# A second two-layer token group goes to seven products for eight, in halves of 256 tokens

## Chip, cores and metric

The kernel runs on one core of one Trainium2 chip. The metric is device time in microseconds of one execution. Three timed executions of the kernel before gave 1100.1, 1101.35 and 1101.55 us; their median is 1101.35 us. One more execution was profiled, and every row below is from that one.

## What is computed

Attention over 4 batches, 8 heads, 576 tokens and 64 columns per head, with scores under (row maximum − tau) left out, and then two dense layers over 2304 tokens of width 512, each with 2048 hidden columns:

```python
def reference(**kwargs):
    attn_out = _attn_ref(**attn_kwargs)
    x = attn_out.transpose(0, 2, 1, 3).reshape(B * S, H * D)
    h = x @ w_in                                      # layer 1
    g = np.where(h >= 1, h, np.where(h <= -1, 0.0, (h + 1) ** 2 / 4))
    x = g @ w_out
    h = x @ w_in2                                     # layer 2
    g = h * np.clip(h + 3.0, 0.0, 6.0) / 6.0
    return g @ w_out2
```

## The kernel before

Everything is held as pairs: an fp32 value is split into a high part (fp32r) and the rest, "low" (`wih`/`wil`, `xh`/`xl`, `gh`/`gl`), and each product of two values is three matmuls (high·high, high·low, low·high). The tokens lie in five groups: four of 512 (one per batch, 0 to 3) and one of 256 (group 4, the last 64 tokens of each batch). The attention and most of layer 1 run first; the change lies in layer 2, from about 716 us on.

Layer 2 before has these stages, in order:

1. Plain groups: `dense(1, 3, ...)` over groups 3, 4 and 0 (`order3`), 16 blocks f of 128 hidden columns each. A step is an input product of 12 matmuls (`em_h`, L725), the gate on ScalarE and VectorE, the split of the gate's result into `gh` (ScalarE) and `gl` (GpSimd), and, two steps later, the output product, 24 matmuls for 512 tokens and 6 for group 4 (`em_out`, L767). `ahead3` puts the layer's weight loads and weight sums beside the steps.
2. The pair: `unit()`. Groups 1 and 2 are the two column halves of one matrix product; two blocks f make its row halves and 256 of the 512 input columns its inner halves. So 2x2 blocks are multiplied with seven products for eight (`PRODUCTS`, L1362: 7 products of 6 matmuls of 512 columns for each of 8 pairs p of blocks). Their left sides are the weights' blocks and sums of them, which `combine` makes in stage 1 and stores to DRAM (`sd`); `fetch` brings them back through a ring of 12 tiles. Their right sides (`combos`, `xw`) are made by `prepare` and lie where the layer's input weights lay. ScalarE copies partial results out of the PSUM banks (`p1`, `U2`, `U3`), VectorE adds the rest (`C11`, `C21`, `C22`, `C12`), and the gate follows. Group 1's gate results go on to its output product (`outs_of`, L1165, one pair of blocks behind); group 2's are stored to DRAM (`rd2`). Beside that, `weight_sums` makes sums of the output weights and stores them (`td`).
3. The last group's output: group 2's output product is done with seven products for eight too (`out_product`, L1300, 336 matmuls of 256 columns). Its left sides come from `rd2` (`load_pair`, `sum_pair`, `high_pair`, `low_pair`), its right sides from `td` (`fetch_sum`, 32 loads).

A scheduler orders the instructions of each engine from the order of the code and a cost model of its own; `after` adds an order (`pins`). Each engine then works through its instructions in that order. Nearly all transfers are issued by SyncE, in its own order.

## Time and profile before

| what | value |
|---|---|
| median of three timed executions | 1101.35 us (1100.1 to 1101.55) |
| the profiled execution: its time | 1102.58 us |
| its span, first to last instruction | 1100.8 us |
| granted TensorE clock, mean | 0.992 of full speed |
| TensorE matmul busy | 1067.0 us (97%) |
| VectorE, ScalarE, GpSimd busy | 740.7, 656.6, 454.0 us |
| moved by DMA | 140.97 MB |

Busy times are shares of the span; a matmul's end is modelled, so matmuls overlap in the rows: what a stream of them costs is read from the chain's rows, where a piece "2.72 us, x12" is twelve starts in a row.

### The profile page before, as it was taken

The page shows a single profiled execution, that of the slowest core. Times are in us where ns is not written, and L with a number is a line of the kernel's source. Part 1 is how long each engine was busy: PE and PEld are TensorE (multiplying, and loading weights), DVE is VectorE, ACT ScalarE, POOL GpSimd, SP SyncE. Part 2 cuts the span into 40 slices and gives each one's busy share as a digit, 9 for nine tenths or more (in the row PEclk, how much of TensorE's full clock was granted, in tenths as well). Part 3 has the DMA queues.
Part 4 walks back from the last instruction along what each step waited for, and adds up shares of the span by engine and source line. Part 5 has one row for each costly group of instructions (what it writes and reads, how often), then busy time and mean ns, then how long its engine had stood idle before and what let it go on. Part 6 is the DMA issues. An engine that isn't in the chain of part 4 may idle for free.

```text
span 1100.8 us, 18826 instructions
## 1 busy us (share of the span) xinstructions
PE 1067.0 (97%) x6658; PEld 882.2 (80%) x6658; DVE 740.7 (67%) x1432; ACT 656.6 (60%) x1304; POOL 454.0 (41%) x390
## 2 busy tenths in 40 slices
PE   7988889999999999999999999999999999999998
PEld 5555567777888888888889888888898888888888
DVE  5899887976676757256536755458565655778766
ACT  5777887776766767465556666645544333544542
POOL 0233667742222322146636665567723222211242
PEclk9999889999999999999999999999999999999999
DMA  6454446233222221015323555655244412877891
GB/s 170 117 98 101 117 118 149 64 75 88 70 66 66 45 61 44 30 50 172 94 73 125 164 178 164 212 169 154 77 154 151 136 58 67 269 259 250 279 348 39
DMA packets 178190, 140.97 MB, mean 128 GB/s; under 512 B 103088, under 2 KB 144304, under 8 KB 178096
## 3 DMA queue, kind: packets, MB, share of 16 engines
q1 hardware_dynamic: 176176, 138.95, 43.3%
q8 instruction: 52, 0.85, 0.3%
q10 hardware_dynamic: 1920, 0.82, 0.3%
q14 instruction: 42, 0.34, 0.1%
HBM read 93.00 MB, written 46.73 MB: 127 GB/s over the span
## 4 chain that ended last, share of the span: by engine, by line
PE 83%; DVE 8%; DMA 3%; ACT 2%; issue 1%; POOL 1%; SPq 1%; DVEq 0%; ACTq 0%; POOLq 0%
PE Q L725 27%; PE P L767 20%; PE Q L787 7%; PE Q L1362 6%; PE Q L482 6%; PE P L381 5%; PE Q L295 4%; PE P L1165 3%; DVE p L396 3%; DVE p L418 2%; PE P L1300 2%; PE Q L1300 1%; DMA tw<-td 1%; DVE xl L706 1%; SPq L234 1%
## 5 line engine op out<-in xcount | busy, mean ns | idle before, releaser
L743 POOL TENSOR_TENSOR gl<-r,gh 128x256 fp32r<-128x256 f32 (+1 forms) x158 | 167.1, 1058 | 324.6 <-ACT gh L742 312.2
L725 PE MATMUL Q<-xh,wih 128*128 128x256 f32 (+1 forms) x632 | 211.8, 335 | 2.6 <-DVE r L736 2.3
L725 PE MATMUL Q<-xl,wih 128*128 128x256 f32 (+1 forms) x632 | 207.3, 328 | 0.0
L725 PE MATMUL Q<-xh,wil 128*128 128x256 f32 (+1 forms) x632 | 207.2, 328 | 0.0
L736 DVE SCALAR_TENSOR_TENSOR r<-r,Q 128x256 f32<-128x256 f32 (+1 forms) x110 | 54.8, 498 | 124.6 <-ACT r L735 120.8
L418 DVE SCALAR_TENSOR_TENSOR p<-p,th,e 128x576 f32<-128x576 f32 x144 | 127.7, 909 | 15.8 <-ACT e L409 10.0
L725 PEld LDWEIGHTS Q<-xh,wih 128*128 128x128 f32 x632 | 120.1, 190 | 21.0 <-DVE r L736 4.1
L742 ACT ACTIVATE gh<-r 128x256 fp32r<-128x256 f32 (+1 forms) x158 | 79.6, 504 | 86.6 <-DVE r L736 31.1
L409 ACT ACTIVATE e<-p,nm 128x576 f32<-128x576 f32 x144 | 109.4, 775 | 36.2 <-DVE p L396 35.3
L725 PEld LDWEIGHTS Q<-xl,wih 128*128 128x128 f32 x632 | 120.2, 190 | 10.9
L725 PEld LDWEIGHTS Q<-xh,wil 128*128 128x128 f32 x632 | 120.1, 190 | 10.3
L295 PE MATMUL Q<-ident,p 128*128 128x128 f32 x656 | 107.3, 281 | 12.8 <-ACT Gf L446 9.7
L295 PEld LDWEIGHTS Q<-ident,p 128*128 128x128 f32 x656 | 74.0, 141 | 42.4 <-ACT Gf L446 16.1
L144 POOL TENSOR_TENSOR w_c<-w_c,w_raw 128x512 int32<-128x512 int32 x64 | 89.5, 1399 | 39.9 <-DVE w_c L142 20.6
L381 PE MATMUL P<-kt,qt 64*128 64x288 f32 (+2 forms) x508 | 82.8, 412 | 10.1 <-DVE p L396 8.1
L446 ACT ACTIVATE Gf<-Q 128x512 f32<-128x512 f32 x128 | 74.2, 595 | 15.8 <-PE Q L295 15.1
L1362 PE MATMUL Q<-xw,sw 128*128 128x512 f32 x336 | 81.0, 390 | 0.0
L396 DVE TENSOR_SCALAR_CACHE_REDUCE p<-P 128x576 f32<-128x576 f32 x90 | 65.2, 751 | 18.9 <-PE Q L295 11.9
L734 ACT ACTIVATE r<-Q,half 128x256 f32<-128x256 f32 (+1 forms) x110 | 58.5, 534 | 32.2 <-PE Q L725 25.3
L787 PE MATMUL Q<-gh,woh 128*128 128x256 f32 x240 | 75.3, 314 | 1.4 <-DVE ob L800 1.4
L1362 PEld LDWEIGHTS Q<-xw,sw 128*128 128x128 f32 x336 | 62.9, 188 | 13.6 <-DVE C L1388 0.7
L482 PE MATMUL Q<-Gf,vn 128*64 128x320 f32 (+1 forms) x512 | 72.8, 423 | 0.1
(199 smaller groups left out, 2454.5 us busy)
## 6 DMA issues: line engine op xcount, KB each, us to landing
w_raw<-in_moe_w_in_dram SPq DMA_DIRECT2D x32, 512.0 KB
w_raw<-in_moe_w_out_dram SPq DMA_DIRECT2D x32, 512.0 KB
sw<-sd SPq DMA_DIRECT2D x56, 256.0 KB
sd<-wz SPq DMA_DIRECT2D x32, 256.0 KB
td<-tz SPq DMA_DIRECT2D x16, 512.0 KB
tw<-td SPq DMA_DIRECT2D x32, 256.0 KB
vn<-in_v_dram SPq DMA_DIRECT2D x32, 128.0 KB
x2p<-ob SPq DMA_DIRECT2D x16, 256.0 KB
```

Of the source, the lines that this page charges most:

```text
L144: x = G.tensor_tensor(out=c.bitcast(I32), in0=c.bitcast(I32), in1=r, op=ALU.add)
L295: x = T.transpose(out, in_, ident)
L381: mm = T.matmul(o, a[j][r, cs], w[j][r, k0:k0 + HS], start=(n == 0), stop=(n == len(terms) - 1), skip_group_check=True)
L396: reads(V.tensor_scalar(out=p[:, x], in0=s[:, :, 0:HS], scalar1=taus[:, 3:4] if j >= JR else -1.0, scalar2=3e38, op0=ALU.mult, op1=ALU.min ...
L409: pins["S"] = S.activation(out=e, in_=p[:, x], func=ACTF.Exp, bias=nm[:, x:x + 1], scale=-1.0)
L418: pins["M"] = V.scalar_tensor_tensor(out=p[:, x], in0=p[:, x], scalar=th[:, x:x + 1], in1=e, op0=ALU.is_le, op1=ALU.mult, accum_out=zt[j][ ...
L482: mm = T.matmul(o[h * D:(h + 1) * D], vn[j % 2][:, c, h, :], f[:, h, c] if c < 4 else t, start=(c == 0), stop=(c == 4), skip_group_check=True)
L725: mm = T.matmul(h, l[:, kk * 128:(kk + 1) * 128], r, start=(x == 0), stop=(x == 3 * KD - 1))
L743: y = G.tensor_tensor(out=gl, in0=r, in1=f32(gh), op=ALU.subtract)
L767: T.matmul(a, l, r, start=(first and x == 0), stop=(last and x == 2))
L787: mm = T.matmul(o, l, r, start=(f == fs[0] and x == 0 and i == 0), stop=(f == fs[-1] and x == 2 and i == 1), skip_group_check=True)
L1362: mm = T.matmul(banks[role], t[:, l, c, :], r, start=(first and y == 0), stop=(y == 5), skip_group_check=True)
```

## The change

Group 0 leaves the plain groups and becomes a second run of the unit, `unit(True)`, behind the pair: its two halves of 256 tokens are the two column halves. Its products have 256 columns (`combos2`, `xz`, made by `small_load` and `small_step` beside the pair's last blocks). The three groups change roles at the output: groups 1 and 2 are now multiplied plainly (group 2's gate results are read back from `rd2` by `again`, split, and multiplied beside group 0's products), and group 0's gate results, stored as `rd3`, take the seven output products at the end. The weight sums of the first two pairs of blocks are made in front, beside group 3 (`EARLY`), those of the other six beside the pair, with their low parts on GpSimd; the sums' source is a copy in DRAM (`ed`) that ScalarE's queue stores when the weights are split. The output weights' sums are made beside the second unit, low parts on GpSimd; those of pairs 0 to 5 stay on the chip (`home`), and only pairs 6 and 7 go through `td`. `fin_out` lets ScalarE evict the even blocks.

```diff
+    ed = [dram.tile([128, 512], F32, name=f"ed{f}") for f in range(KF)]
+    rd3 = [dram.tile([128, MAIN], F32, name=f"rs{f}") for f in range(KF)]
...
         x = S.activation(out=hi, in_=f32(c), func=ACTF.Copy)
         after(x, pins["S"])
+        if (kind, m) == ("i", 1):
+            nc.scalar.dma_start(out=ed[f], in_=f32(c))
...
     def fin_out(g, a, i):
-        if i % 2:
+        if i % 2 == 0:
             S.activation(out=ob, in_=a, func=ACTF.Copy, scale=1.0 / 6.0)
...
-    order3 = [NB - 1, NB, 0]
+    order3 = [NB - 1, NB]
+    G0 = 0
...
+    def small_part(k, c, t):
+        hi, lo = combos2[c, XN[k]] = small_tile(k, c)
+        paced(S.activation(out=hi, in_=t, func=ACTF.Copy), "S")
+        minus(lo, t, f32(hi))
+    def small_load(c):
+        raw2[c] = [wide["p"].tile([128, MAIN], F32, tag="xst", name="ty", bufs=3) for _ in range(3)]
+        for t, kk in zip(raw2[c], (c, 2 + c)):
+            nc.sync.dma_start(out=t, in_=x2d[G0][:, kk, :])
...
-    def weight_sums():
+    def weight_sums(ps):
+        def home(p):
+            n = 2 + 2 * p if p < 6 else 2 * p - 10
+            return [[place_of(n + x, hl, F32R, "tw") for hl in "hl"] for x in range(2)]
...
-                minus(z[:, 1, :], t, f32(z[:, 0, :]))
-                nc.sync.dma_start(out=f32(td[p])[:, n], in_=f32(z))
+                rounded_off(lo, t, hi, False)
+                for x, t in enumerate((hi, lo)):
+                    if p < 6:
+                        tw[p, 2 * n + x] = t
+                    else:
+                        nc.sync.dma_start(out=f32(td[p])[:, n, x], in_=f32(t))
...
-    def unit():
+    def unit(second, between):
+        n = 256 if second else MAIN
+        xs_of = combos2 if second else combos
...
+            def sink(t, row, col):
+                if second:
+                    r = t[:, 256:512]
+                    S.activation(out=r, in_=t[:, 0:256], func=ACTF.Relu, bias=three)
+                    pins["V"] = V.scalar_tensor_tensor(out=r, in0=r, scalar=6.0, in1=t[:, 0:256],
+                                                       op0=ALU.min, op1=ALU.mult)
+                    nc.sync.dma_start(out=rd3[(f0, f1)[row]][:, 256 * col:256 * col + 256], in_=r)
+                elif col:
+                    nc.sync.dma_start(out=rd2[(f0, f1)[row]], in_=gate(t))
+                else:
+                    gg[(f0, f1)[row]] = parts(gate(t))
+            p1 = copy("p1", product(0, 0), n)
+            sink(add("C11", product(1, 1), p1, n), 0, 0)
+            outs(0)
+            u2 = copy("U2", product(2, 0, False), n)
+            c21 = product(4, 2)
+            outs(1)
+            u3 = copy("U3", product(3, 0, False), n)
+            sink(add("C21", u3, c21, n, ALU.subtract), 1, 0)
+            sink(add("C22", product(5, 3), u3, n), 1, 1)
+            outs(2)
+            outs(3)
+            sink(add("C12", product(6, 3, False), u2, n), 0, 1)
+            between(p, 7)
...
+    def again(f):
+        r = ringed("r", F32)
+        nc.sync.dma_start(out=r, in_=rd2[f])
+        hh[f] = parts(r)
+    def beside_first(p, k):
+        if k < 7:
+            next(late, 0)
+        if p == last_p - 2 and k == 7:
+            small_load(0)
+        elif p == last_p - 1 and k < 6:
+            small_step(k + 1, 0)
...
+    def beside_second(p, k):
+        if k in (2, 4):
+            again(2 * p + (k == 4))
+        if p < last_p:
+            next(sums_of, 0)
+            if k == 7 and p == last_p - 1:
+                load_pair(0)
+                load_pair(1)
+                for n in range(5):
+                    fetch_sum(n)
+            return
...
+    first_sums = in_turn(range(EARLY), True)
+    late = in_turn(range(EARLY, KF // 2), False)
+    sums_of = weight_sums((6, 7, 0, 1, 2, 3, 4, 5))
...
-    unit()
+    unit(False, beside_first)
+    unit(True, beside_second)
+    last_group()
```

What stands in each engine's row of work shows it at three places. `Q` and `P` are PSUM banks, `sw` the fetched weight blocks.

TensorE, in layer 2: before, one step of group 0, an input product and the output products two steps behind.

```order
L725 MATMUL Q_10521<-xl,wih_8940 128x512
L725 MATMUL Q_10521<-xh,wil_8941 128x512
L767 MATMUL P_10151<-woh_8815,gh 128x512
L767 MATMUL P_10151<-wol_8816,gh 128x512
L767 MATMUL P_10151<-woh_8815,gl 128x512
```

And now, in the second unit, the start of one pair of blocks: two products of 256 columns, a part of group 2's output, and two more products, the first into the bank that the first product left.

```order
L1443 MATMUL Q_11852<-xz,sw 128x256 x6
L1443 MATMUL Q_11869<-xz,sw 128x256 x6
L1227 MATMUL P_11455<-woh_8404,gh 128x512
L1227 MATMUL P_11455<-wol_8405,gh 128x512
L1227 MATMUL P_11455<-woh_8404,gl 128x512
L1227 MATMUL P_11455<-woh_8536,gh 128x512
L1227 MATMUL P_11455<-wol_8537,gh 128x512
L1227 MATMUL P_11455<-woh_8536,gl 128x512
L1443 MATMUL Q_11852<-xz,sw 128x256 x6
L1443 MATMUL Q_11907<-xz,sw 128x256 x6
```

Group 0's 192 input matmuls of 512 columns became 336 of 256; all other counts in layer 2 stay (384 of 512 columns at L1165 and L767 for the outputs of two groups are now at L1227).

GpSimd, in the pair before (all of it rests of gate results):

```order
L1154 TENSOR_TENSOR gl_11413<-r_11409,gh_11412 128x512
L1154 TENSOR_TENSOR gl_11499<-r_11495,gh_11498 128x512
L1154 TENSOR_TENSOR gl_11555<-r_11551,gh_11554 128x512
L1154 TENSOR_TENSOR gl_11641<-r_11637,gh_11640 128x512
L1154 TENSOR_TENSOR gl_11691<-r_11687,gh_11690 128x512
```

And at the start of the second unit, where `gl_11319`, `11357`, `11473`, `11512` are the rests of group 2's blocks f = 0 to 3 and `gl_11618` that of f = 4:

```order
L1216 TENSOR_TENSOR gl_11319<-r_11316,gh_11318 128x512
L1216 TENSOR_TENSOR gl_11357<-r_11354,gh_11356 128x512
L1095 TENSOR_TENSOR tw_11361<-te_11279,tw_11360 128x512
L1095 TENSOR_TENSOR tw_11363<-te_11292,tw_11362 128x512
L1216 TENSOR_TENSOR gl_11473<-r_11470,gh_11472 128x512
L1216 TENSOR_TENSOR gl_11618<-r_11615,gh_11617 128x512
L1216 TENSOR_TENSOR gl_11512<-r_11509,gh_11511 128x512
L1095 TENSOR_TENSOR tw_11490<-te_11424,tw_11489 128x512
```

The low parts of the weight sums (`tw`) stand between the rests, and block 3's rest stands behind block 4's.

ScalarE, where the last pair of blocks begins: before, the last group's first split (`gt`) stood behind the copies `p1` and `U2` of that pair.

```order
L1147 ACTIVATE r_11725<-C12_11723,three_75 128x512
L1383 ACTIVATE p1_11760<-Q3_11753 128x512
L1147 ACTIVATE r_11778<-C11_11776,three_75 128x512
L1383 ACTIVATE U2_11809<-Q3_11753 128x512
L1153 ACTIVATE gh_11781<-r_11778 128x512
L1259 ACTIVATE gt_11799<-r2_11735 128x256
```

Now it stands ahead of both, and of the gate of `C12` of the pair of blocks before.

```order
L1215 ACTIVATE gh_12334<-r_12332 128x512
L1325 ACTIVATE gt_12351<-r2_12274 128x256
L1215 ACTIVATE gh_12374<-r_12372 128x512
L1470 ACTIVATE C12_12268<-C12_12268,three_75 128x256
L1415 ACTIVATE p1_12299<-Q3_12292 128x256
L1325 ACTIVATE gt_12352<-r2_12275 128x512
L1470 ACTIVATE C11_12315<-C11_12315,three_75 128x256
L1325 ACTIVATE gz_12354<-gs_12310 128x512
L1415 ACTIVATE U2_12340<-Q3_12292 128x256
```

`r2_12274` is a tile that SyncE reads from `rd3`; until it has landed, ScalarE does nothing that stands behind `gt_12351`.

## Rows read from the trace of the kernel before

**Rows 1.** The page's first part and its clock slices (fortieths of the span).

```profile
span 1100.8 us, 18826 instructions
...
PE 1067.0 (97%) x6658; PEld 882.2 (80%) x6658; DVE 740.7 (67%) x1432; ACT 656.6 (60%) x1304; POOL 454.0 (41%) x390
...
PEclk9999889999999999999999999999999999999999
```

**Rows 2.** Stretches: us; busy PE, PEld, DVE, ACT, POOL; clock; DMA share; GB/s.

```profile
716.10:797.40 81.30, 81.30 (x359) 66.90 (x358) 52.04 (x60) 41.82 (x70) 57.12 (x43) 1.00 0.44 134
797.40:844.70 47.30, 47.30 (x299) 42.85 (x299) 27.51 (x54) 19.52 (x43) 13.81 (x16) 1.00 0.42 135
844.70:930.00 85.30, 85.30 (x378) 70.62 (x378) 52.79 (x74) 33.39 (x56) 23.01 (x17) 1.00 0.32 101
930.00:1049.60 119.60, 119.60 (x527) 98.59 (x526) 87.55 (x133) 57.25 (x96) 25.06 (x19) 1.00 0.78 259
1049.60:1096.80 47.20, 46.52 (x361) 44.87 (x359) 32.74 (x51) 15.79 (x30) 19.12 (x15) 1.00 0.52 188
```

**Rows 3.** Chain that ended last, in order of time: start us, us, what.

```profile
875.30 2.72 PE Q L725 x12
...
990.90 5.44 PE Q L1362 x24
...
1072.69 4.32 PE P L1300 x36
```

**Rows 4.** Groups by form, TensorE, 844 to 932 us (group 0's plain steps).

```profile
L725 PE MATMUL Q<-xh,wih 128*128 128x512 f32 x64 | 24.9, 389 | 0.0
```

**Rows 5.** TensorE in order of time at the start of the last output.

```profile
1057.59 0.28 PE L1300 MATMUL Q<-wol,gh 128*128 128x256 f32 x1
1058.40 0.38 PE L1300 MATMUL Q<-woh,gl 128*128 128x256 f32 x1 [0.53 <-POOL gl L1267]
...
1059.29 0.50 PE L1165 MATMUL P<-woh,gh 128*128 128x512 f32 x1 [0.15 <-DVE ob L830]
```

**Rows 6.** Groups by form, ScalarE, 700 to 1100 us.

```profile
L1193 ACT ACTIVATE tz<-ts 128x512 fp32r<-128x512 f32 x16 | 9.5, 625 | 10.8 <-DVE ts L1091 10.8
L1383 ACT ACTIVATE U<-Q 128x512 f32<-128x512 f32 x16 | 9.5, 591 | 17.2 <-PE Q L1362 17.2
...
L738 ACT ACTIVATE r<-Q,three 128x256 f32<-128x256 f32 x16 | 7.5, 471 | 13.4 <-PE Q L725 10.0 <-POOL gl L743 3.4
```

**Rows 7.** Groups by form, VectorE, 700 to 1100 us.

```profile
L1179 DVE TENSOR_TENSOR te<-woh,wol 128x512 f32<-128x512 f32 x16 | 13.8, 890 | 0.0
...
L1091 DVE TENSOR_TENSOR ts<-te 128x256 f32<-128x256 f32 x16 | 8.4, 552 | 0.0
...
L739 DVE SCALAR_TENSOR_TENSOR r<-r,Q 128x256 f32<-128x256 f32 x16 | 6.7, 417 | 15.6 <-ACT r L738 15.6
```

**Rows 8.** Groups by form, GpSimd, 700 to 1100 us.

```profile
L1154 POOL TENSOR_TENSOR gl<-r,gh 128x512 fp32r<-128x512 f32 x16 | 21.9, 1370 | 94.5 <-ACT gh L1153 78.6 <-PE Q L1362 15.9
```

**Rows 9.** Chain that ended last: the transfers on it behind 1030 us.

```profile
1036.96 6.60 DMA tw<-td
1043.57 5.51 DMA tw<-td
1049.16 6.67 DMA r<-rr
```

**Rows 10.** Stretches again: three with many transfers.

```profile
620.00:630.00 10.00, 10.00 (x50) 8.37 (x49) 7.09 (x11) 7.44 (x15) 7.36 (x6) 1.00 0.51 151
960.00:970.00 10.00, 10.00 (x46) 8.29 (x45) 8.64 (x15) 4.60 (x8) 2.85 (x2) 1.00 0.93 332
...
1060.00:1070.00 10.00, 10.00 (x71) 9.32 (x70) 4.46 (x9) 3.72 (x7) 3.58 (x3) 1.00 1.03 379
```

**Rows 11.** The page's DMA issues: loads of weight blocks, KB each.

```profile
sw<-sd SPq DMA_DIRECT2D x56, 256.0 KB
```

**Rows 12.** Weight blocks' issue on SyncE: ns, shortest/median/longest.

```profile
L1132 SPq DMA_DIRECT2D sw<-sd x56: 319/352/1397, 842.8 to 1023.6; - x56
```

More of the change, by code (lines that the diff above doesn't have):

```diff
@@ L1386, in add @@
-            def add(name, x, y, op=ALU.add):
-                t = place_of(14 + (name[2] == "2"), "hl"[name[1] == "2"], F32, name)
-                V.tensor_tensor(out=t, in0=x, in1=y, op=op)
-                return t
-            def outs(i):
-                if p:
-                    for f in (2 * p - 2, 2 * p - 1):
-                        outs_of(G1, accs, i, f, gg[f], pins["T"] if p == last_p else None)
-            def store(r, f):
-                nc.sync.dma_start(out=rd2[f], in_=r)
-            if p == last_p:
+                elif not second:
+                    fetch(0, w)
@@ new lines, in product, with outs @@
+                between(p, turn[0])
+                turn[0] += 1
+                return banks[role]
+            def outs(i):
+                q = p - 1
+                if q < 0 and second:
+                    q = last_p
+                    i = (0, 2, 1, 3)[i]
+                if q >= 0:
+                    g, a = (G2, hh) if second and p else (G1, gg)
+                    for f in (2 * q, 2 * q + 1):
+                        outs_of(g, accs, i, f, a[f], pins["T"] if second and p >= 2 else None)
```

246 lines of the change are left out of this document (145 added, 101 removed).

## The prediction, made before the changed kernel ran

> **What bounds the kernel now.** I read the page's head first, then busy time by stretch, then the chain of waits. The reader is to see that TensorE is the bound of everything the change touches: 97% of the span over all, and the granted clock is at full speed, 2.4 GHz, in all slices behind the first few [rows 1]. By stretch, TensorE is busy 333.5 of 333.5 us from the start of layer 2 to the end of the pair, and 46.52 of 47.20 us in the last output [rows 2]. VectorE (52.0 of 81.3, 87.6 of 119.6), ScalarE and GpSimd have room in each. So an edit here is worth what it takes from TensorE's row of work, less what it makes TensorE wait. A busy matmul is no measure of its cost, since matmuls overlap; the chain gives the distance of their starts. Twelve matmuls of 512 columns take 2.72 us and 24 take 5.44, so 0.2267 us each, in plain groups and in the pair alike; 36 of 256 columns take 4.32, so 0.120 us each [rows 3]. Two matmuls of 256 columns cost 0.240 and not 0.2267: halving the columns costs 13 ns per matmul of 512 columns' worth of work.
>
> **TensorE's work.** Group 0's input products leave: 3 x 64 = 192 matmuls of 512 columns [rows 4], 192 x 0.2267 = 43.52 us. In come 8 rounds (a round is one pair of hidden blocks) of 7 products of 6 matmuls of 256 columns: 336 x 0.120 = 40.32 us. The output products keep their counts: the groups only change roles. The sum is **-3.20 us**. So an eighth less arithmetic is 7.4% less time, since the columns are halved. That 192 became 336 is seen in the order of the changed kernel, so that the change does not do what it says is no rival here.
>
> The rows' price stands against a rule. The Trainium skill, "TensorE: Matmul & The Clock Gate", section "Back-to-back issue gap", gives for a stream of weight loads and matmuls a sustained distance of 81 ns at 128 columns and 131 ns at 512. On a line between them 256 columns would take 98 ns (an estimate from that page), and the change would cost 336 x 0.098 - 192 x 0.131 = +7.8 us. The trace disagrees with the page: 0.2267 us at 512 columns. I take the rows' prices, both measured in this kernel with a weight load for each matmul.
>
> **What must stay hidden in the second unit.** A round there takes 42 x 0.120 + 24 x 0.2267 = 10.48 us of TensorE, where the pair's takes 66 x 0.2267 = 14.96. Per round:
> - ScalarE: 3 copies at no more than 0.591, 4 gates at 0.471, and 2 + 8/7 x 2 = 4.3 splits at 0.625 [rows 6]: 6.4 us.
> - VectorE: 4 additions and 4 gates at about 0.417, and 8/7 weight sums of 2 x 0.890 + 4 x 0.552 [rows 7]: 7.9 us.
> - GpSimd: 4.3 rests at 1.370 [rows 8]: 5.9 us; the weight sums' rests moved to it from VectorE.
> - SyncE: 13 issues, 17 in the first two rounds, at 0.352 us [rows 12]: 4.6 to 6.0 us.
>
> All fit in 10.48 us. The third product writes into the bank that the copy `p1` must have left; one product and six output matmuls lie between, 0.72 + 1.36 = 2.08 us, for a copy of at most 0.591. The last product waits for the addition `C22`, with 2.72 us of output matmuls between. Cost: 0, hidden by output matmuls; without them each would show its 0.6 us.
>
> **Transfers.** A tile is 256 KB, 0.262 MB [rows 11]. A round of the second unit moves 7 weight blocks, 2 tiles read back and 4 half tiles stored: 11 tiles, 2.88 MB, 275 GB/s. The first two rounds add 4 tiles each of weight sums: 3.93 MB, 375 GB/s. What the 16 engines can do is the rate over the busy share: 151/0.51 = 296, 332/0.93 = 357, 379/1.03 = 368 GB/s [rows 10]. So the first two rounds end 1 us late at 357 GB/s and 5.6 us late at 296. The ring of weight blocks is fetched up to 12 products ahead (11 x 1.5 = 16 us, less a landing of under 7), which hides that. Two loads have less room:
> - Group 2's block 3 is read back behind the store of a weight sum whose rest GpSimd makes in round 2. By the rows that rest is done 0.72 + 0.59 + 0.63 + 1.37 = 3.3 us into the round, and with three issues on SyncE the read starts at about 4.2. Split (0.63) and rest (1.37) must be done behind two products and five output matmuls of round 3 (1.44 + 5 x 0.2267 = 2.57 us), so it must have landed by 10.48 + 2.57 - 2.0 = 11.05: **6.9 us** are allowed.
> - `r2_12274` holds up ScalarE ahead of the last round's `p1`. It is issued behind the store of `C11`, some 1.44 + 0.42 + 0.47 + 0.42 + 0.35 = 3.1 us into round 7. Two splits, a gate and the copy `p1` stand on ScalarE from it on, at most 0.63 + 0.63 + 0.47 + 0.59 = 2.3 us, and `p1` is due 2.80 us into round 8: it must land by 10.48 + 2.80 - 2.3 = 11.0, so **7.9 us** are allowed.
>
> The three landings on the chain, with the engines at a share of 1.0, took 5.51 to 6.67 us [rows 9]. No row shows such a load in the new traffic; bounds are 5.5 and, with the backlog of 5.6 added, 12.3 us. I take 6.67, the nearest, so both loads cost 0, but with 0.2 and 1.2 us to spare.
>
> **Beside the plain groups.** Group 3's stretch moved 134 GB/s x 81.3 us = 10.9 MB [rows 2]; stores of the plain weight blocks (32 tiles), part of the copies `ed`, and two early sums add about 13 MB, making some 298 GB/s, close to the lowest of the three rates. Weights are split two steps (10.9 us) ahead of their use at the tightest, so lateness of a few us costs 0. ScalarE's 16 issues of `ed`, some of which stand until an earlier transfer has landed, lie in stretches where a gate has 10.9 us until its output product. `prepare` moves into group 4's 47.3 us, adding 22 VectorE instructions of at most 0.89 (19.6 us) to 27.5 busy, from which four weight sums (about 16 us) leave: 31 of 47.3, cost 0. In the pair, 6 sums with rests on GpSimd take the place of 8 with rests on VectorE: VectorE gets lighter, cost 0. The swap in `fin_out` is an exchange of 0.59 and 0.68 us evictions, cost 0. The end behind the last matmul is as before.
>
> **Sum.** The profiled execution took 1102.58 us, 1.8 over its span: less 3.20 it is 1099.4. It stands 1.2 above the median of the runs, 1101.35; by the median the forecast is **1098.2 us**. A measurement can tell about 0.2%, 2.2 us, from no change, so this is a gain by one microsecond more than can be told.
>
> **Rivals.**
> 1. *The join gets better too.* The last output now starts with 8 loads of weight sums in place of 32, and TensorE's idle 0.68 us there [rows 2], most of it a wait of 0.53 for a rest on GpSimd [rows 5], may go. Against it: such rests are still made there. 1097.5 us. Chance 0.06.
> 2. *Loads land moderately late.* For: 375 GB/s is asked of engines that did 296 to 368. Each us beyond 6.9 is lost once, beyond 7.9 twice. Landing in 7.9 to 10.1 us: 1.0 to 5.4 us lost, 1099.2 to 1103.6 us, about no change. Against: from round 3 on the demand is 275, and later reads run a round or more ahead. Chance 0.33.
> 3. *Late loads decide: slower.* The same two places, from a landing of 10.1 us on, where (10.1 - 6.9) + (10.1 - 7.9) = 5.4 us eat the gain and 2.2 more. At 12.3 us it is 5.4 + 4.4 = 9.8 lost: 1108.0 us. For: SyncE's queue is in order, and a store that waits for a gate holds up reads behind it. Against: TensorE lost nothing in the pair at 259 GB/s. Chance 0.16.
> 4. *Short matmuls are dearer in the unit than in the last output.* The gain is gone at 43.52 / 336 = 0.1295 us each; at 0.150 the time is 1098.2 + 336 x 0.030 = 1108.3. Against it stand 36 in a row at 0.120 [rows 3]. Chance 0.02; the rule above points this way.
>
> **How the numbers follow.** Forecast as it stands 0.43, with rival 1 it is 0.49 for faster by over 0.2%; rival 2 is the 0.33 within; rivals 3 and 4 are the 0.18 slower. The range starts below rival 1, by the 1.25 us that the lowest run lies under the median, at 1096.3, and ends where rival 3 begins, rounded, at 1103.5; that leaves out rivals 3 and 4 and little else.
>
> **What would show it right or wrong.** Right: a stretch of 84 us behind the pair with TensorE busy throughout, twelve starts of 256 columns in 1.44 us, and layer 2 shorter by 3 us. Wrong by rival 2 or 3: idle of TensorE before a third product at `p1`, or before output matmuls released by GpSimd's `gl` in the first rounds of the second unit, and transfers of over 7 us on the chain. Wrong by rival 4: a distance of starts over 0.13 us with no wait. Idle in group 3's stretch behind weight splits would show that I priced the moved stores wrongly.

## The result, and the profile after

The changed kernel takes **1112.84 us** (median of 4 runs, 1111.32 to 1112.99). The kernel before, beside it on the same chip, takes 1100.72 us (4 runs, 1098.65 to 1101.55). The ratio is 1.0110, with a 95% interval of 1.0092 to 1.0127: slower by 12 us, where 3 us less were forecast.

Profiled was the fastest of its runs, 1111.32 us, span 1109.5, while the profiled run of the kernel before, 1102.58 with a span of 1100.8, was slower than its four timed ones. So the two traces lie only 8.7 us apart. Another 2.2 us lie ahead of what follows: the trace of before comes to the last layer-1 steps at 614.55 us and this one at 612.31, with 17.1 us of half granted clock before them for 10.2. The head of its page (busy time, then the shares of the chain that ended last):

```profile
PE 1065.1 (96%) x6802; PEld 884.1 (80%) x6802; DVE 735.0 (66%) x1454; ACT 668.5 (60%) x1354; POOL 485.3 (44%) x418
...
PE 65%; DVE 16%; DMA 6%; issue 5%; ACT 4%; POOL 3%; SPq 1%; DVEq 0%; ACTq 0%; POOLq 0%
```

TensorE is busy for about the time it was [rows 1], but the chain now runs through other engines for 35% of the span, for 17% before. The stretches that answer to [rows 2], with the same columns: group 3, group 4, pair, second unit, last output.

```profile
716.00:799.70 83.70, 81.42 (x356) 66.05 (x355) 57.31 (x71) 42.35 (x72) 56.38 (x42) 1.00 0.65 200
799.70:847.50 47.80, 47.80 (x302) 43.22 (x301) 23.20 (x40) 21.88 (x49) 13.32 (x16) 1.00 0.27 88
847.50:963.40 115.90, 115.89 (x512) 95.68 (x511) 61.73 (x104) 53.93 (x95) 36.14 (x28) 1.00 0.78 254
963.40:1055.90 92.50, 87.51 (x536) 77.10 (x535) 76.08 (x127) 47.64 (x103) 51.01 (x39) 1.00 0.92 307
1055.90:1105.20 49.30, 46.50 (x362) 44.88 (x360) 30.05 (x52) 15.40 (x28) 12.85 (x11) 1.00 0.24 76
```

The clock is full in all of them. Three stretches have TensorE idle: group 3 (2.3 us), the second unit (5.0), the last output (2.8). TensorE's waits by what it waited for, from 600 us on (us in total, times, longest):

```profile
PE P L1366 <- DVE ob L834: 2.4, 2, 1.4
PE P L1227 <- ACT ob L832: 2.3, 2, 2.0
PE P L771 <- POOL gl L747: 2.3, 2, 1.4
PE Q L1443 <- ACT U L1415: 1.8, 2, 1.5
PE Q L1443 <- DVE C L1420: 1.2, 2, 0.8
```

No one of them is large, and no DMA is among them. The idle time leaves out what a stopped pipeline costs at its new start. So from here on a loss is counted in starts: what the distance from one matmul to the next exceeds 0.2267 us (512 columns) or 0.120 us (256) by, over all gaps of more than 0.04 us. Such a count is good to some 0.3 us a stretch, since a gap between a long and a short matmul can be priced in more than one way. Counted so, TensorE loses 4.6 us from the start of the last layer-1 steps at 612 us to group 4, nothing in group 4, 0.3 in the pair, 6.5 in the second unit and 3.6 in the last output: 15.0, where the trace of before has 1.9 (0.3, 0, 0.4, 1.2). Without these losses the same stretches went from 480.1 to 477.9 us. So most of the forecast saving is there, 2.2 of 3.2 us, and 13.1 us of new waits stand against it: together the 10.9 by which the two traces differ from these steps on.

**Group 3.** From the timeline, the rows of VectorE, GpSimd and TensorE around its first loss (start, us, engine, line; in brackets the idle time before and what ended it):

```profile
757.31 1.78 DVE L1102 TENSOR_TENSOR wz<-ws,wz 128x512 fp32r<-128x512 f32 x1
759.02 0.68 DVE L144 SCALAR_TENSOR_TENSOR w_c<-w_raw,w_c 128x512 uint32<-128x512 uint32 x1
...
759.78 1.31 POOL L146 TENSOR_TENSOR w_c<-w_c,w_raw 128x512 int32<-128x512 int32 x1 [1.23 <-DVE w_c L144]
761.04 1.72 POOL L747 TENSOR_TENSOR gl<-r,gh 128x512 fp32r<-128x512 f32 x1
...
762.82 0.50 PE L771 MATMUL P<-woh,gl 128*128 128x512 f32 x1 [1.43 <-POOL gl L747]
```

One row of ScalarE's waits from 612 to 800 us (us in total, times, longest):

```profile
ACT w_c L134 <- DMA ed<-w_c: 13.9, 7, 3.5
```

A low part of an early weight sum (`wz`) runs on VectorE ahead of the split's next step (L144), so GpSimd's step of the split (L146) starts 1.23 us late, and the gate's low part `gl`, behind it on GpSimd, is what TensorE stands for. The row of waits shows the other hold: the store `ed` reads the tile `w_c`, of which there are two, and ScalarE's next split may not write it before the store has landed.

**The join of the pair and the second unit.** From the timeline, ScalarE's rows and then TensorE's:

```profile
970.65 0.50 ACT L1470 ACTIVATE C<-C,three 128x256 f32<-128x256 f32 x1
973.50 0.63 ACT L1215 ACTIVATE gh<-r 128x512 fp32r<-128x512 f32 x1 [2.35 <-DMA r<-rr]
974.04 1.07 ACT L832 ACTIVATE ob<-P 128x512 f32<-128x512 f32 x2
...
974.67 0.50 PE L1227 MATMUL P<-woh,gh 128*128 128x512 f32 x1 [1.96 <-ACT ob L832]
```

ScalarE stands 2.35 us for block 1's read-back, and the two evictions of group 1's output stand behind it. They are ScalarE's only since the swap in `fin_out`.

**Inside the second unit.** From the timeline, rows of VectorE, then GpSimd, then TensorE:

```profile
1005.86 0.42 DVE L1420 TENSOR_TENSOR C<-Q,p 128x256 f32<-128x256 f32 x1
1007.10 1.54 DVE L1471 SCALAR_TENSOR_TENSOR C<-C 128x256 f32<-128x256 f32 x1 [0.82 <-ACT C L1470]
1008.56 0.68 DVE L1247 TENSOR_TENSOR te<-woh,wol 128x512 f32<-128x512 f32 x1
1009.16 0.41 DVE L1420 TENSOR_TENSOR C<-Q,U 128x256 f32<-128x256 f32 x1
...
1010.15 0.42 DVE L1471 SCALAR_TENSOR_TENSOR C<-C 128x256 f32<-128x256 f32 x1 [0.25 <-ACT C L1470]
...
1011.07 1.27 DVE L1471 SCALAR_TENSOR_TENSOR C<-C 128x256 f32<-128x256 f32 x1 [0.16 <-ACT C L1470]
1012.27 1.78 DVE L1247 TENSOR_TENSOR te<-woh,wol 128x512 f32<-128x512 f32 x1
...
1005.81 2.54 POOL L1095 TENSOR_TENSOR tw<-te,tw 128x512 fp32r<-128x512 f32 x2 [1.08 <-ACT tw L1259]
1010.72 2.79 POOL L1216 TENSOR_TENSOR gl<-r,gh 128x512 fp32r<-128x512 f32 x2 [2.36 <-ACT gh L1215]
...
1009.63 2.42 PE L1443 MATMUL Q<-xz,sw 128*128 128x256 f32 x18 [0.49 <-DVE C L1420]
1014.90 0.86 PE L1443 MATMUL Q<-xz,sw 128*128 128x256 f32 x5 [0.75 <-DVE C L1420]
```

The same gate operation of VectorE (L1471) takes 0.42 us at 1010.15, when GpSimd is idle, and 1.54 and 1.27 us when GpSimd works. The additions `C`, which free the banks that TensorE writes next, stand behind it. Over the whole stretch, VectorE's groups by form (busy us, mean ns of one):

```profile
L1471 DVE SCALAR_TENSOR_TENSOR C<-C 128x256 f32<-128x256 f32 x31 | 24.1, 786 | 7.7 <-ACT C L1470 7.7
L1102 DVE TENSOR_TENSOR te<-te 128x256 f32<-128x256 f32 x32 | 18.6, 581 | 0.6
L1247 DVE TENSOR_TENSOR te<-woh,wol 128x512 f32<-128x512 f32 x16 | 13.8, 886 | 0.0
```

The gate's mean is nearly twice the 0.42 us that it takes undisturbed.

**The last output.** A row of VectorE's timeline:

```profile
1066.66 0.43 DVE L1300 TENSOR_TENSOR gs<-r 128x256 f32<-128x256 f32 x1 [4.68 <-DMA r<-rs]
```

And a row of the waits of SyncE's queue, 1048 to 1070 us:

```profile
SPq L1290 <- DMA rs<-C: 3.9, 2, 3.2
```

VectorE stands 4.68 us for pair 3's load, with the evictions `ob` (L834) behind it. SyncE had issued that load behind the loads of pair 7, which wait until the last store of the unit has landed.

### The profile page after: what moved, and what is told of

It reads as the page before. It is cut to its first block, busy times and chain, and to the rows that moved or that the text cites. A ratio compares the mean times of both kernels' runs of the same rounds, so it can differ in the third digit from the quotient of the medians.

```text
span 1109.5 us, 19529 instructions
## 1 busy us (share of the span) xinstructions
PE 1065.1 (96%) x6802; PEld 884.1 (80%) x6802; DVE 735.0 (66%) x1454; ACT 668.5 (60%) x1354; POOL 485.3 (44%) x418
## 4 chain that ended last, share of the span: by engine, by line
PE 65%; DVE 16%; DMA 6%; issue 5%; ACT 4%; POOL 3%; SPq 1%; DVEq 0%; ACTq 0%; POOLq 0%
PE Q L729 17%; PE P L771 11%; PE Q L1443 8%; PE Q L791 7%; PE P L385 5%; PE Q L486 5%; PE P L1227 4%; PE Q L299 4%; DVE p L400 3%; DVE p L422 2%; DMA ed<-w_c 2%; PE P L1366 1%; POOL w_c L146 1%; DVE w_c L138 1%; PE Q L1366 1%
## 5 line engine op out<-in xcount | busy, mean ns | idle before, releaser
L747 POOL TENSOR_TENSOR gl<-r,gh 128x256 fp32r<-128x256 f32 (+1 forms) x142 | 142.6, 1005 | 258.3 <-ACT gh L746 240.2
L729 PE MATMUL Q<-xh,wih 128*128 128x256 f32 (+1 forms) x568 | 187.2, 329 | 3.4 <-DVE r L740 3.2
L729 PE MATMUL Q<-xl,wih 128*128 128x256 f32 (+1 forms) x568 | 182.6, 321 | 0.0
L729 PE MATMUL Q<-xh,wil 128*128 128x256 f32 (+1 forms) x568 | 182.5, 321 | 0.0
L422 DVE SCALAR_TENSOR_TENSOR p<-p,th,e 128x576 f32<-128x576 f32 x144 | 124.7, 887 | 16.6 <-ACT e L413 11.0
L729 PEld LDWEIGHTS Q<-xh,wih 128*128 128x128 f32 x568 | 108.2, 191 | 19.4 <-DVE r L740 5.1
L729 PEld LDWEIGHTS Q<-xl,wih 128*128 128x128 f32 x568 | 108.3, 191 | 8.4
L729 PEld LDWEIGHTS Q<-xh,wil 128*128 128x128 f32 x568 | 108.2, 191 | 8.1
L746 ACT ACTIVATE gh<-r 128x256 fp32r<-128x256 f32 (+1 forms) x142 | 69.4, 490 | 69.0 <-DVE r L740 38.4
L146 POOL TENSOR_TENSOR w_c<-w_c,w_raw 128x512 int32<-128x512 int32 x64 | 89.0, 1391 | 49.4 <-DVE w_c L144 27.3
L1216 POOL TENSOR_TENSOR gl<-r,gh 128x512 fp32r<-128x512 f32 x32 | 43.8, 1375 | 100.3 <-ACT gh L1215 85.5
```

Source lines behind the costliest of these rows:

```text
L146: x = G.tensor_tensor(out=c.bitcast(I32), in0=c.bitcast(I32), in1=r, op=ALU.add)
L422: pins["M"] = V.scalar_tensor_tensor(out=p[:, x], in0=p[:, x], scalar=th[:, x:x + 1], in1=e, op0=ALU.is_le, op1=ALU.mult, accum_out=zt[j][ ...
L729: mm = T.matmul(h, l[:, kk * 128:(kk + 1) * 128], r, start=(x == 0), stop=(x == 3 * KD - 1))
L747: y = G.tensor_tensor(out=gl, in0=r, in1=f32(gh), op=ALU.subtract)
```

## The experiments

Eighteen runs. Each kernel is the changed one with the edit shown. Losses are in starts, as above, from one profile each; where two medians are compared, the ratio to the kernel before goes with each. The changed kernel's own interval is 1.0092 to 1.0127. Only e2, e16 and e17 lie clear of it on the faster side, and e4, e8, e12 and e18 on the slower; what another edit does is read from its trace.

The counts hold one thing more than waits. In eleven of the eighteen profiles (e1, e4, e6, e8 to e11, e13, e14, e17, e18) the granted clock of TensorE falls from full to half inside layer 2, 17 times in all, for 3.4 us each, which costs 1.5 to 1.7 us each time and is counted in the losses. Each time TensorE had just stood still, or still stood, for 1.6 to 3.9 us in one piece; but in e3, e7 and e12 it stood for 2.0 to 2.2 us and the clock stayed full. The changed kernel's profile has no such fall in layer 2. So a wait at one place can cost more in one kernel than in another, and a small difference between two totals is no proof of a cause.

**e1: who issues the stores `ed`.**

```
-            nc.scalar.dma_start(out=ed[f], in_=f32(c))
+            nc.sync.dma_start(out=ed[f], in_=f32(c))
```

> The sixteen copies ed are issued by SyncE and not by ScalarE; all else stays. Theory A (ScalarE stands at an issue of ed until an earlier transfer has landed, and the weight splits and gates behind it come late): the stretch up to the end of group 3 loses about 4 us less, so some 1108.5 us in place of 1112.8. Theory B (the added transfers themselves make the weights late there): no change, 1112 to 1113 us. The second unit loses as much as before under both.

1113.4 us, ratio 1.0118 [1.0101, 1.0136]; 4.8 us lost before group 4. It is not the issuing queue.

**e2: no sums of the output weights.**

```
+    def plain_sums(ps):
+        for p in ps:
+            for n in range(2):
+                for x in range(2):
+                    tw[p, 2 * n + x] = wsp["o", 1, 2 * p + n][x]
+        yield
-    sums_of = weight_sums((6, 7, 0, 1, 2, 3, 4, 5))
+    sums_of = plain_sums(range(KF // 2))
```

(`fetch_sum` returns at once.)

> The sums of the output weights are left out in the second unit, with their stores and loads (the split output weights themselves stand in their place, so the last group's output is another value; TensorE's work is the same). Theory C (GpSimd's low parts of these sums, and the sums themselves, hold VectorE up, and VectorE's additions out of the PSUM banks come late): the second unit's waits of TensorE on VectorE and on the copies, about 4 us, go, so about 1108.5 us; VectorE's instructions that took 1.2 to 1.5 us beside GpSimd take 0.42. Theory D (the read-backs from DRAM land late and stand in front of these): at most 1 us from lighter transfers, 1111.5 to 1113 us.

1107.18 us, ratio 1.0067 [1.0050, 1.0084]. The second unit loses 3.0 us for 6.5, 2.1 of it at the join. The sums, with their stores and loads, are worth some 3.5 us there.

**e3: loads of pairs 3 to 7 in order.** In `load_pair`:

```
+            x = nc.sync.dma_start(out=t, in_=rd3[f])
+            if p >= 3:
+                after(x, pins.get("L"))
+                pins["L"] = x
```

> Only SyncE's order changes: the loads of pairs 3 to 7 for the last output are issued in the order of the pairs, so that pair 3's load no longer stands behind pair 7's, which waits for the last store. Theory E (pair 3's load lands late behind the last store, VectorE waits 4.7 us for it with two evictions of PSUM banks behind it): the last output loses 2 to 2.5 us less, about 1110.5 us. Rival: the load is bound by its tile (pair 1 must be done with it) and nothing is won, 1112 to 1113 us.

1110.29 us, ratio 1.0091 [1.0076, 1.0106]. The last output loses 1.7 us for 3.6, and the row of VectorE's timeline that answers to the one above is:

```profile
1062.84 0.83 DVE L1303 TENSOR_TENSOR gs<-r 128x256 f32<-128x256 f32 x1 [1.38 <-DMA r<-rs]
```

The wait is 1.38 us for 4.68. The five kernels with this order (e3, e10, e13, e16, e17) lose 1.0 to 1.7 us in the last output, the other thirteen 1.9 to 7.2. So about 2 of the 3.6 us are the order of the loads; 1.2 were lost there before the change too.

**e4: read-back one pair of blocks earlier.**

```
-        if k in (2, 4):
-            again(2 * p + (k == 4))
+        if k in (2, 4) and p < last_p:
+            again(2 * p + 2 + (k == 4))
...
     unit(False, beside_first)
+    again(0)
+    again(1)
```

> Group 2's gate results are read back one pair of blocks earlier. Theory D (late read-backs: block 1's lands late and ScalarE waits 2.35 us for it, with the evictions of group 1's output behind it): 2 to 3 us less, about 1110 us, and the wait of 2 us before the second unit's output matmuls is gone. Theory C (VectorE held up by GpSimd): that wait alone is gone or moved, the others stay, 1110.5 to 1113 us.

1116.65 us, ratio 1.0148 [1.0133, 1.0163]. The join's wait stayed (2.1 us), the unit lost 13.2, 3.1 of it at half clock. The read-back of block 1 lands no earlier: SyncE issues it at the same place, behind a wait for GpSimd's `gl`, which still reads the tile.

**e6: the low parts of the output sums on VectorE.**

```
-                rounded_off(lo, t, hi, False)
+                rounded_off(lo, t, hi, True)
```

> The 16 low parts of the output weights' sums on VectorE instead of GpSimd. Theory C (GpSimd's two-operand work stretches VectorE's from 0.4 to 1.3 us and so makes the sums of the products late): the second unit falls from 92.5 to 90 to 91 us though VectorE gets some 16 x 0.55 = 9 us more work, and the time is 1110 to 1112 us. Theory D (VectorE simply has too much to do there, 76 of 92.5 us): the unit grows to 93 to 95 us, 1113 to 1116 us.

1109.49 us, ratio 1.0092 [1.0068, 1.0117]. The unit loses 3.2 us, 2.1 of it at the join. Its stretch, columns as above:

```profile
963.80:1052.60 88.80, 86.09 (x535) 77.21 (x534) 75.93 (x142) 47.72 (x102) 28.71 (x21) 1.00 0.95 318
```

VectorE does 16 operations more, 16 x 0.68 = 10.9 us by their undisturbed time, and its busy time is the same, 75.93 for 76.08 us. So nearly 11 us of its 76 were time in which these operations on GpSimd held it. The gate's mean fell from 0.786 to 0.655 us. GpSimd went from 51.01 to 28.71 us. Theory C holds for the unit; the time alone, with its interval, does not tell e6 from the changed kernel; the last output lost 5.3 us for 3.6, 1.5 of it at half clock.

**e7: the swap in `fin_out` undone.**

```
-        if i % 2 == 0:
+        if i % 2:
             S.activation(out=ob, in_=a, func=ACTF.Copy, scale=1.0 / 6.0)
```

> One part of the change undone: ScalarE evicts the odd token tiles of an output again, VectorE the even ones first. Theory H (at the join ScalarE stands for block 1's read-back with the evictions of group 1's output behind it, 2.1 us of TensorE): that wait falls under 0.7 us, 1110 to 1111.5 us. Rival (VectorE, which makes the sums of the products, is the worse place for the first evictions, and the last output loses more than the join gains): 1112.5 to 1115 us.

1111.65 us, ratio 1.0111 [1.0093, 1.0129]. The wait at the join is there still, 1.67 us, now for VectorE's eviction, which stands behind the sums of the output weights; the unit loses 8.2 us, and the ratio is the changed kernel's. Who evicts is no cure by itself.

**e8: no stores `ed`.** The stores are gone; the first sums add both halves on VectorE, the late ones load both from `sd` and add them:

```
+            for t, f in zip(ex, (2 * p, 2 * p + 1)):
+                hi, lo = wsp["i", 1, f]
+                paced(V.tensor_tensor(out=t, in0=f32(hi), in1=f32(lo), op=ALU.add), "V")
...
+            for t, lo in zip(ex, lows):
+                paced(V.tensor_tensor(out=t, in0=t, in1=lo, op=ALU.add), "V")
```

> The 16 stores of the put-together weights are left out, and with them what reads the tile of the split; the sums of the first two pairs of blocks add the halves on VectorE (4 more operations of about 0.9 us), the late ones load both halves from where they stand for the combinations (12 more loads of 256 KB beside the pair) and add them. Theory F (the store holds one of the two tiles in which a weight is put together, and ScalarE's next split stands for it, 13.9 us in 7 waits): the stretch from 612 to 800 us falls from 187.4 to 183 to 184.5 us, the pair stays at 116 to 117 us, and the time falls from 1112.8 to 1108.5 to 1110 us. Rival G (the splits two steps ahead are too much there, whatever the store does): 187 us still, 1112 to 1114 us.

1124.49 us, ratio 1.0214 [1.0199, 1.0230]. A miss: 5.9 us lost before group 4, 3.6 in the pair, where 0.3 had been, 10.2 in the unit and 6.2 in the last output (3.0 of these two at half clock). Between 612 and 716 us, where the changed kernel loses 1.1 us and no sums run, nothing is lost now. But that tells nothing of the stores: e6 and e15, which keep them, lose nothing there either. Behind 716 us, where VectorE got busier, more is lost. So VectorE's work alone can hold the splits up; what the store does e12, e14 and e18 have to show.

**e9: at the join, evictions ahead of block 1.**

```
+            pins["F"] = S.activation(out=ob, in_=a, func=ACTF.Copy, scale=1.0 / 6.0)
...
         hh[f] = parts(r)
+        if f == 1:
+            after(pins["S"], pins["F"])
```

> One order pinned: at the join ScalarE rounds block 1's read-back behind its two evictions of group 1's output instead of ahead of them. Theory H, narrowed (the evictions stand behind a load that lands at 973.5 us; undoing who evicts only moved the wait to VectorE): TensorE's 2.0 us at the first output product go to under 0.5 us, and the time falls to 1110.3 to 1111.5 us. Rival (the block's halves then come late for the next output products, and the wait moves there): 1112.3 to 1113.5 us.

1116.16 us, ratio 1.0143 [1.0119, 1.0168]. The 2.1 us at the join are gone, and the unit loses 7.5 us all the same, 3.5 of it near 1011 us: 2.05 behind a gate that was held 1.54 us beside GpSimd, and behind that 1.4 at half clock (columns as above):

```profile
1011.60:1015.00 3.40, 3.40 (x18) 3.30 (x17) 3.11 (x6) 1.37 (x3) 1.60 (x3) 0.50 0.88 280
```

And the last output loses 7.2 us for 3.6, half of it in one wait behind a load (a row of ScalarE's and one of TensorE's) and 1.5 at half clock:

```profile
1069.18 0.42 ACT L1325 ACTIVATE gt<-r 128x256 fp32r<-128x256 f32 x1 [5.37 <-DMA r<-rs]
...
1072.28 0.50 PE L1227 MATMUL P<-woh,gh 128*128 128x512 f32 x1 [3.50 <-ACT ob L832]
```

The wait at the join moved, as the rival said, though not to the next output products.

**e10: e8, e3, e6 and e9 together.**

> Together: no stores of the put-together weights, loads of pairs 3 to 7 in order, the low parts of the output weights' sums on VectorE, the evictions at the join ahead of block 1. If the four losses are separate and add up: 1112.8 - 3 to 4 (group 3) - 2.5 (last output) - 3.3 (second unit) - 1.5 to 2 (join) = 1100 to 1102.5 us, that is level with the kernel before, with group 3 at 183 to 184.5, the second unit at 86 to 88 and the last output at 47 to 48 us. Rival (they are one shortage of VectorE and ScalarE time that shows at another place when one is mended): 1104 to 1107 us.

1116.65 us, ratio 1.0143 [1.0122, 1.0163]: 6.3 lost before group 4, 4.4 in the pair, 6.5 in the unit, 1.0 in the last output; 3.1 of it all at half clock. Only e3's part came through. The losses before group 4 and in the pair are those of e8.

**e11: two output sums beside the pair.** For pairs 6 and 7 the rounded halves lie in the stage's tiles, and

```
             next(late, 0)
+            if p in (1, 2):
+                next(sums_of, 0)
```

> Two of the eight output weight sums (pairs 6 and 7, which go by way of memory in any case) are made beside the pair, where VectorE is busy 61.7 of 115.9 us, instead of at the head of the second unit. Theory C/D (the sums' work on VectorE and GpSimd is what makes the second unit's products late; leaving all of it out took its loss from 6.5 to 3.0 us): the second unit falls from 92.5 to 90 to 91.7 us, the pair stays at 116 us, the time 1110.3 to 1112 us. Rival (one shortage that shows elsewhere, as where the evictions were put ahead): the pair or the last output grows by as much, 1112.3 to 1114 us.

1110.6 us, ratio 1.0088 [1.0073, 1.0103]. The unit lost 6.0 us, 3.4 of it at the join, which grew; inside, the losses fell from 4.4 to 2.6, of which 1.7 are half clock right behind the join. So the waits inside the unit fell to 0.9 us.

**e12: the first input sums later.**

```
-        if n >= 4:
-            next(first_sums, 0)
+        if n >= KF - 3:
+            for _ in range({KF: 4, KF + 1: 5}.get(n, 1)):
+                next(first_sums, 0)
```

> The sums of the input weights' first two pairs of blocks are made at the end of group 3 and the head of group 4, when no weight is split any more, instead of beside group 3's splits. Theory K (it is VectorE's extra work there, 57.3 against 54.7 us of 84, and 64.0 with a larger loss where it also added the halves, that makes the split and so GpSimd's low parts late): group 3's losses of 1.6 and 1.0 us near 761 and 785 us go, the stretch falls from 187.4 to 184 to 185.5 us, 1110 to 1111.5 us. Rival F2 (the store of the put-together weight alone, which holds the split's tile): 187 us still, 1112 to 1113.5 us.

1116.5 us, ratio 1.0148 [1.0128, 1.0168]. Theory K alone falls: 3.7 us are still lost before group 4, and group 4 loses 2.6 new ones behind VectorE's evictions, which stand behind an operation that waited 3.24 us for the stores of these sums. The profiled execution is the fastest of its runs, 1113.15 us.

**e13: e11, e12, e6 and e3 together.**

> Together: the two moves of sums (two output sums beside the pair, the first input sums behind the splits), the low parts of the output sums on VectorE, and the loads of pairs 3 to 7 in order. If the losses are of single places and the moves add up: 1112.8 - 2 - 3.3 - 1 - 2.5 = 1103 to 1105.5 us, still slower than before (1100.7). Rival (one shortage): 1107 to 1111 us.

1109.76 us, ratio 1.0088 [1.0074, 1.0101]: the rival's range. Of the unit's loss of 5.0 us, 2.4 are the join and 1.7 half clock; group 4 loses 4.3, 1.6 of it at half clock.

**e14: the stores of blocks 4 to 15 made in group 4.**

```
-        if (kind, m) == ("i", 1):
+        if (kind, m) == ("i", 1) and f < 4:
...
+        if 1 <= k <= 12:
+            hi, lo = wsp["i", 1, k + 3]
+            t = wide["p"].tile([128, 512], F32, tag="io", name="ew", bufs=3)
+            paced(V.tensor_tensor(out=t, in0=f32(hi), in1=f32(lo), op=ALU.add), "V")
+            nc.sync.dma_start(out=ed[k + 3], in_=t)
```

> Twelve of the sixteen stores of the put-together weights are taken out of the split (those of blocks 4 to 15) and made in group 4 from the two halves, added on VectorE into a tile of the evictions' pool (12 additions of 0.7 to 0.9 us where VectorE is busy 22.9 of 47 us). The sums beside group 3 stay as they are. Theory F (the store holds the split's tile): the stretch from 612 to 800 us falls from 187.4 to 183 to 184.5 us, group 4 stays at 47.8, the time 1108.5 to 1110.5 us. Theory F+K (store and sums each suffice to delay a split chain that has no slack): 185.5 to 187.5 us still, 1111.5 to 1114 us.

1112.06 us, ratio 1.0102 [1.0087, 1.0118]; 3.8 us lost before group 4. To take away the stores alone, or the sums alone (e12), does not help.

**e18: e14's and e12's edits together. e19: e14's, and the 32 stores of the halves moved too:**

```
-        if n < KF:
-            plain(n)
+        if n >= KF:
+            plain(n - KF)
```

> Both taken out of group 3's stretch: the stores of blocks 4 to 15 made in group 4, and the first sums at the end of group 3 and the head of group 4. Theory F+K (in the kernel before, one split's round of GpSimd, ScalarE and GpSimd again took about 5.0 us in group 3 against 5.44 us of TensorE work per block, and either the store or the sums take these 0.44 us away): the stretch from 612 to 800 us is 183 to 184 us, though group 4 may lose 2 to 3 us at its head by the sums in one burst. Rival L (the 32 stores of the halves for the combinations, which this kernel has in group 3 and the one before has not, hold the weights' loads on SyncE's queue and the DMA engines): 186 to 187 us still.

> The 32 stores of the halves for the combinations moved from group 3 to group 4, together with the stores of the put-together weights of blocks 4 to 15; the first sums stay beside group 3. Theory F+K (the sums on VectorE and ScalarE suffice to take the split chain's 0.44 us per block): the stretch from 612 to 800 us stays at 186 to 187 us. Rival L (it is these stores): 183 to 184 us.

Stretches, columns as above: in e18 that from 612 us to group 4, and group 4 with what it lost:

```profile
612.00:795.00 183.00, 183.00 (x818) 151.28 (x817) 112.85 (x147) 108.25 (x187) 119.03 (x90) 1.00 0.54 169
795.00:850.00 55.00, 49.85 (x302) 44.52 (x301) 35.93 (x60) 23.57 (x52) 17.95 (x16) 0.97 0.55 190
```

And in e19 that up to group 4:

```profile
612.50:798.90 186.40, 183.85 (x818) 151.19 (x817) 120.78 (x155) 110.00 (x190) 118.59 (x89) 1.00 0.58 180
```

With store and sums both gone TensorE is busy throughout, 183.00 us, the length that this stretch has before (182.9). With the halves' stores gone and the sums left it is 186.40. So F+K holds and L falls: store and sums each suffice. The split's last rounds show why. GpSimd's step of the split (L144 before, L146 after) starts at 754.17 and, seven rounds later, at 789.10 us in the trace of before, at 751.80 and 786.72 in e18: 34.9 us both. In e14 it is 753.99 to 791.27, 37.3; in e12 751.96 to 790.30, 38.3. Seven blocks take TensorE 7 x 5.44 = 38.1 us (12 input and 12 output matmuls each; the 24 output matmuls named for a step further above are 12). So the splits had 0.46 us a block to spare, and have next to none with the store or the sums beside them. That the lead with which they enter group 3 is then used up at its end is read from these times; it was not varied by itself.

e18 took 1116.19 us all the same, ratio 1.0148 [1.0133, 1.0163], since group 4 loses 7.3 us there. From the timeline, two rows of VectorE's and one of GpSimd's:

```profile
811.47 0.69 DVE L1102 TENSOR_TENSOR tx<-tx 128x512 f32<-128x512 f32 x1 [5.15 <-DMA sd<-wz]
812.08 0.68 DVE L834 TENSOR_SCALAR ob<-P 128x512 f32<-128x512 f32 x1
...
824.29 5.29 POOL L747 TENSOR_TENSOR gl<-r,gh 128x256 fp32r<-128x256 f32 x2 [5.02 <-PE Q L729]
```

VectorE stands 5.15 us for the stores of the sums just made, with the eviction behind it that TensorE waits for: 3.5 us. Two low parts on GpSimd take 5.29 us beside VectorE's additions, where one takes 0.74 alone: 2.0 us. And 1.6 us are half clock. e19 took 1110.06 us, ratio 1.0099 [1.0078, 1.0120].

**e15: e9's order with e6's low parts.**

> The evictions at the join ahead of block 1's read-back, together with the low parts of the output sums on VectorE. Alone the first took the 2.1 us at the join away, but the second unit lost 7.5 us for 6.5 all the same; alone the second took the unit's loss to 3.2 us, 2.1 of it at the join. Theory C (what came in place of the join's wait was VectorE held by GpSimd's two-operand work): now the unit loses only 1 to 2 us (87 to 88 us) and the time is 1107 to 1109 us. Rival (ScalarE's evictions first make block 1's halves late for the next output products, whoever makes the sums): the unit loses 3 to 5 us, 1109 to 1112 us.

1109.62 us, ratio 1.0083 [1.0070, 1.0096]; the unit loses 3.7 us, about as much as with e6 alone (3.2), and the last output 4.5. 1.5 us are lost near 986 us, behind these rows of the timeline, VectorE's and then GpSimd's:

```profile
983.38 1.51 DVE L1471 SCALAR_TENSOR_TENSOR C<-C 128x256 f32<-128x256 f32 x1
984.82 1.33 DVE L1102 TENSOR_TENSOR te<-te 128x256 f32<-128x256 f32 x3
986.15 0.42 DVE L1420 TENSOR_TENSOR C<-Q,U 128x256 f32<-128x256 f32 x1
...
982.80 1.81 POOL L1216 TENSOR_TENSOR gl<-r,gh 128x512 fp32r<-128x512 f32 x1 [3.42 <-ACT gh L1215]
```

The rival's loss came, by another way: a gate held by the block's own low part, then three operations of a weight sum, and the addition that TensorE waits for behind them. VectorE's three rows follow each other without a pause.

**e16 and e17: the best of these: e14, e6 and e3, with and without e9's order.**

> Together: stores of blocks 4 to 15 in group 4, low parts of the output sums on VectorE, loads of pairs 3 to 7 in order, evictions at the join first. By the single losses: 1112.8 - 3 (group 3) - 3.3 - 1.5 (second unit, join) - 2.5 (last output) = 1102.5 us, range 1100 to 1106 us.

> The same without the order of the evictions at the join: 1112.8 - 3 (group 3) - 3.3 (second unit) - 2.5 (last output) = 1104 us, range 1101 to 1107 us.

1106.24 us (e16), ratio 1.0046 [1.0033, 1.0059]; 1107.68 us (e17), ratio 1.0058 [1.0045, 1.0071]. e16 is the fastest of all eighteen and still slower than the kernel before: 3.8 us are lost before group 4, 3.5 in the unit, 1.6 in the last output. In e17 the unit loses 4.1, of which 2.1 are the join and 1.5 the half clock right behind it. No kernel here beats the one before.

## Why the prediction was wrong

**TensorE's work: right, but for 1 us.** Outside the losses the 256-column matmuls of the second unit start 0.120 us apart, as in the last output, so the fourth rival falls. Of 3.20 us 2.2 are found.

**"All fit in 10.48 us": the step that failed first.** The sum of an engine's durations against the round's length was taken as cover. VectorE was put at 7.9 us a round, 63 us in eight. It was busy 76.08 us. The additions came as priced (0.41 us), and so did the weight sums (0.886 and 0.581 us for 0.890 and 0.552). The gate did not: 0.786 us for 0.417, 24.1 us in all for 13. Its price was that of group 4's gate, L739 [rows 7], which reads one operand from PSUM, and the unit's gate has both in SBUF. Such operations wait beside GpSimd, which e6 puts at nearly 11 us over all of VectorE's, and GpSimd worked 51.01 of 92.5 us here, for 25.06 of 119.6 in the pair before the change [rows 2]. Some 13 us of other work in this stretch (the pair's last gates, `xz`, evictions, the first sums of the last output) stood in no sum. And a round is no pool of time: an addition `C` has 2.72 us of matmuls to hide in, a gate of 1.5 us and a weight sum of 0.7 us ahead of it on the queue use that up. e2, which takes the sums out, gives back 3.5 of the unit's 6.5 us; e6, which moves their low parts, 3.3.

**"The swap in `fin_out` is an exchange, cost 0": wrong in its place.** What the price left out is the queue: ScalarE's evictions stood behind a read-back at the join, 2.1 us. Undoing the swap (e7) left a wait there; turning the order (e9) ended it, and other places lost more.

**"ScalarE's 16 issues of `ed`" and "lateness of a few us costs 0" in group 3: wrong.** The prediction priced the issue and not what a store holds: the tile it reads, for up to 3.5 us at a time. And it took the lead of two steps as slack for every engine, when the lead is used up at the end of group 3. By e12, e14 and e18 store and early sums each suffice for 3.7 us. The traffic that was feared there, 298 GB/s, was 200. That idle time in group 3's stretch would show this was named, and so it showed.

**The late loads (rivals 2 and 3): the right kind, at other places.** The size, 1107 to 1108 us, is not far off, but block 3's read-back, where 6.9 us were allowed, stopped TensorE nowhere. The second tight load did in part: ahead of the last round ScalarE stood 1.45 us for a load of the last output's first pairs, then 1.36 us for VectorE, and 1.6 us were lost. What decided in the last output was the order on SyncE: pair 3's load behind pair 7's (about 2 us, e3), which the prediction did not look at, because it took "the end behind the last matmul" and the last output as before.

**The join better (rival 1): the reverse.** Fewer loads did stand in the last output (0.24 of the DMA engines' time for 0.52 [rows 2]), and it became 2.1 us longer.

What stays open: with the sums' low parts on VectorE and the join's order mended (e15, e16) the second unit still loses 3.5 to 3.7 us for the pair's 0.3, in pieces of 0.3 to 1.5. That gates held by GpSimd and sums ahead of additions make it up is read from the traces, not tried one by one. Nor was it found out why the granted clock fell behind some waits and not behind others. A third tile for the split was not tried, for want of space.

## What to carry to other kernels

When TensorE is saved work by halving columns, every round gets shorter while the other engines' rounds do not. So check each wait against the matmuls that lie between, in the order of the queue, and not the engines' sums against the round. Take a duration from an operation whose operands lie in the same memories, and count it at the load it will run under: a gate with both operands in SBUF beside a GpSimd at 55% took 0.786 us for the 0.417 of one that reads PSUM. A store holds its source until it has landed, and a lead that is consumed to its end has no slack for anybody.

## What the runs showed of the hardware

**VectorE and GpSimd hold each other up, but only where all of VectorE's operands are in SBUF.** In the second unit the gate's multiplication (L1471, 128x256) took 0.41 to 0.43 us in 13 cases with GpSimd idle. Of the 18 that overlap an operation of GpSimd, 14 took 0.53 to 1.54 us; the other four (0.41 to 0.43) started ahead of GpSimd's next operation or less than 0.1 us before the end of one. `te<-woh,wol` (L1247, 128x512) took 0.67 to 0.69 us alone, and 1.78 in three of four beside GpSimd. The additions with one operand in PSUM (L1420, 128x256) took 0.41 to 0.42 us in 17 cases with GpSimd working, as in 14 without, and an eviction from PSUM took 0.68 both ways. At 1007.10 the gate started just behind GpSimd's second operation and ended 0.3 us after it, at 1008.64. In e18 it was GpSimd that stood: its two low parts of 0.74 us took 5.29 us beside VectorE's additions.

The Trainium skill, "SBUF — State Buffer", section "Summary: rules for kernel authors", says that a VectorE operation with two SBUF inputs and a GpSimd operation that reads SBUF exclude each other, and the one that issues second waits until the first has finished. The trace agrees, in the 0.3 us above and in the additions from PSUM that are not touched.

**A store holds its tile for microseconds.** ScalarE waited 13.9 us in 7 pieces, up to 3.5 us each, for stores of 256 KB that only read the tile it wanted to write.

**TensorE's granted clock can fall to half behind a wait.** In e9 TensorE stood 1.89 us before 1011.0 us and 3.50 us before 1072.3; the granted clock was at half speed, 1.2 GHz, from 1011.6 to 1015.0 and from 1073.0 to 1076.4 us, and full again behind that. The matmuls of 256 columns then started 0.213 us apart for 0.120, and those of 512 columns 0.427 for 0.227.
